# A fused attention and two-block MoE kernel: attention's TensorE order regrouped by shape, two small jobs moved to GpSimd

## The chip, the cores and the metric

The kernel runs on one core of one Trainium2 chip. The metric is the device time of one execution in microseconds, the median of the runs. Before the change it is 554.88 us (three runs, 554.71 to 554.99).

## The reference

```
scores = q @ k.T / 8            # 2 batches x 12 heads, 448 positions, 64 per head
scores = where(causal, scores, -1e9)
attn   = exp(scores - max);  attn = attn / (sum(attn) + 1e-9)
x      = attn @ v               # -> 896 tokens x 768
y      = ((x @ w_a) * (x @ w_b)) @ w_out          # d_ff 1536
h      = y @ w_in;   out = (h / (1 + exp(-h))) @ w_out2   # d_ff 2048
```

All of it is float32.

## The kernel before

The core does attention first (about 0 to 97 us), then the products of the two MoE blocks, which split every float32 operand into a high and a low part.

**Units and half-units.** Attention works on 12 units: unit `u` is a pair of heads of one batch (6 per batch). The 448 query positions of a unit are three blocks of 128 and a last one of 64. The last blocks of both heads share one tile, called `LAST`. A unit is done in two half-units `(u, i)`: half 0 holds block 1 of both heads and `LAST`, half 1 holds blocks 2 and 0 of both heads (`STEPS`). A half-unit goes through four stages:

- `scores` (L622, L631): products of q and k into PSUM tiles `sc`. L622 has 64 rows by 64 columns of weights, four of them side by side in the array. L631 is the product for `LAST`: its weights `q_last` are padded with zeros to 128 rows, by 64 columns. These two stages, in short S(u,i) and L(u), share the PSUM pool `ps_s`.
- `soft`: on VectorE (DVE) one instruction adds mask and scale and takes the row minimum of the negated scores (L646, tile `sm`, four buffers), then ScalarE (ACT) takes the exponential and its row sums (L651, tiles `p`, `sums`).
- `normalize`: DVE adds 1e-9 to the sums (L659) and takes the reciprocal (L660), then GpSimd (POOL) multiplies `p` by it (L663).
- `transposes`, in short T(u,i): eight 128x128 transposes on TensorE (PE) into two PSUM banks `pt` (L694), the first copied out by ACT, the second by DVE (both L782). Then `pv`: PV(u,i) multiplies with v (L705), weights of 128 rows by 64 columns; when a unit is complete, `arrive` makes `xh` (ACT, L390), for batch 1 also `xf` (ACT, L393), and `xl` (DVE, L397).

**What sets the order.** Everything is in the order in which the program issues it. The loop over steps `d` (two per unit) calls per step, before the change, `scores(d)`, then `pv` of half-unit `d - LAG_PV`, then `transposes` of half-unit `d - LAG_T`. What the other engines have to do is put into the table `late` by `defer(k, prio, fn)`, for step `d + k`, and at the end of a step that step's entries are issued in order of `prio`:

```
for _, fn in sorted(late.pop(d, ()), key=lambda e: e[0]):
    fn()
```

Then `line.to` issues the steps of the weights' conversion that are due. The weights of the first two granules (groups of weight blocks) are converted during attention: `exp` (ACT, L220, scales the upper words), `low` (ACT, L226), `join` and `sign` (DVE, L232 and L237), then the high and low parts (ACT L259, DVE L263). In the last steps the first MoE products ("fill", L302, 36 matmuls in four portions) are put between the attention stages. TensorE starts with eight warm-up matmuls (L723), while the first q and k load.

**PSUM.** `ps_s` has three banks for scores, transposes use two banks `ps_t` and one bank `ps_g[1]` in turn, `ps_x` and `ps_g[0]` hold `xo`.

Of the kernel before, what the change touches and what calls it, by code (L numbers as in the profile page):

```python
# [10 lines left out]
F32 = mybir.dt.float32  # L11
# [7 lines left out]
P = 128  # L19
D = 64  # L20
# [48 lines left out]
def fused_kernel(ctx: ExitStack, tc: tile.TileContext, qk, v, w_ab, w_mid, w_in, w_out, out):  # L69
# [122 lines left out]
    def convert(g):  # L192
# [22 lines left out]
        for i in range(2):  # L215


            @step(due["exp"][i])
            def _(i=i):
                nc.scalar.activation(out=word(i, 1).bitcast(F32), in_=word(i, 1).bitcast(F32), func=AF.Copy,  # L220
                                     scale=2.0 ** -112)


            @step(due["low"][i])
            def _(i=i):
                nc.scalar.activation(out=word(i, 0), in_=word(i, 0), func=AF.Relu, bias=wbias, scale=2.0 ** -29)  # L226

            @step(due["join"][i])
            def _(i=i):
                if i == 0:  # L230
                    g["wq"] = wtp.tile([P, 2 * H], F32, tag="wq", name="wq")
                nc.vector.scalar_tensor_tensor(out=xi(i), in0=word(i, 1), scalar=3, in1=word(i, 0),  # L232
                                               op0=ALU.logical_shift_left, op1=ALU.bitwise_or)

            @step(due["sign"][i])
            def _(i=i):
                nc.vector.scalar_tensor_tensor(out=xi(i), in0=word(i, 1), scalar=0x80000000, in1=xi(i),  # L237
                                               op0=ALU.bitwise_and, op1=ALU.bitwise_or)
                R.free(g["raw"][i])
# [295 lines left out]

    for g in granules:
        if g["stage"] == 3 and g["m"] in (0, 2):
            g["due"] = (CONV_X, CONV_Y)[g["m"] // 2]  # L540
        if g["stage"] == 4 and g["m"] == 0 and not g["fast"] and g["k"]:
            g["due"] = CONV_Z
    loads += [(g, src) for g in granules for src in g["src"]]

    with tc.manual_schedule():

        with ExitStack() as actx:
# [47 lines left out]
            def load_qk(u):  # L595
                t = U[u]
                t["qk"] = qk_p.tile([P, 2, S], F32, tag="qk", name="qk")
                nc.sync.dma_start(out=t["qk"], in_=qk[u])
                for h in range(2):
                    r = slice(h * D, (h + 1) * D)  # L600
                    nc.sync.dma_start(out=q_last[u % NQ][r, h, :], in_=qk[u, r, 0, S - D:])

            def load_v(u):
                U[u]["v"] = v_p.tile([P, NKB, P], F32, tag="v", name="v")
                nc.sync.dma_start(out=U[u]["v"], in_=v[u])

            def scores(u, i):


                t = U[u]  # L610
                if i == 0:
                    for n in ("sums", "nmax", "rcp"):
                        t[n] = st_p.tile([P, len(COL)], F32, tag=n, name=n)
                bank = [ps_s.tile([P, 512], F32, tag="s", name="sc") for _ in range(2)]
                q, k = t["qk"][:, 0], t["qk"][:, 1]
                work, o = [], HS if i == 0 else 0
                for n in (1,) if i == 0 else (2, 0):
                    K = P * (n + 1)
                    for h in range(2):
                        r = slice(h * D, (h + 1) * D)  # L620
                        for e in range(2):
                            nc.tensor.matmul(  # L622
                                out=bank[h][e * D:(e + 1) * D, o:o + K], lhsT=q[r, n * P + e * D:n * P + (e + 1) * D],
                                rhs=k[r, 0:K], start=True, stop=True,
                            )
                        work.append(((h, n), [(bank[h][:, o:o + K], mask[:, 3 * P - K:])]))
                    o += K
                if i == 0:
                    for part in range(2):
                        for h in range(2):  # L630
                            nc.tensor.matmul(  # L631
                                out=bank[part][h * D:(h + 1) * D, 0:HS], lhsT=q_last[u % NQ][:, h, :],
                                rhs=k[:, part * HS:(part + 1) * HS], start=True, stop=True,
                            )
                    work.append((LAST, [(bank[0][:, 0:HS], mask[:, 0:HS]), (bank[1][:, 0:HS], mask_last)]))
                for j, src in work:
                    defer(0, 2, partial(soft, u, j, src))
# [30 lines left out]
            def transposes(u, i):  # L668
# [4 lines left out]
                    t["pt"] = pt_p.tile([P, NKB, 2, S], F32, tag="ptr", name="ptr")  # L673
                bank = []
                for _ in range(2):
                    pool, tag = (ps_g[1], "g") if n_banks[0] % 3 == 2 and u < NP + 2 else (ps_t, "t")
                    n_banks[0] += 1
                    bank.append(pool.tile([P, 512], F32, tag=tag, name="pt"))
                o, todo = [0, 0], []
                for n, copy, kb, nkb, blk in COPIES[i]:  # L680
                    w = D if blk == 3 else P
                    size = nkb * 2 * w
                    src = bank[n][:, o[n]:o[n] + size].rearrange("p (k h q) -> p k h q", k=nkb, h=2)
                    o[n] += size
                    dst = t["pt"][:, kb:kb + nkb, :, blk * P:blk * P + w]
                    for a in range(nkb):
                        for j, out_ in [(LAST, src[:, a])] if blk == 3 else [((h, blk), src[:, a, h]) for h in range(2)]:
                            todo.append((out_, p_sb[u % 2][j][:, (kb + a) * P:(kb + a + 1) * P]))
                    if nkb == 1:
                        src, dst = src[:, 0], dst[:, 0]  # L690
                    copy = nc.vector.tensor_copy if copy == "vector" else nc.scalar.copy
                    defer(1, 0, partial(copy, out=dst, in_=src))
                for out_, p in todo:
                    nc.tensor.transpose(out=out_, in_=p, identity=ident)  # L694

            def pv(u, kb):
# [55 lines left out]
            for d in range(n_steps):  # L752
                now[0] = d
                u, i = divmod(d, 2)
                if u == NU and i == 0:
# [4 lines left out]
                    banks.add(ctx.enter_context(right(name="ps_r", bufs=3, space=PSUM, reuse_waits="tile")), 3)  # L760
# [8 lines left out]
                if u < NU:  # L769
                    scores(u, i)  # L770
                u, i = divmod(d - LAG_PV, 2)
                if 0 <= u < NU:
                    for kb in range(2 * i, min(2 * i + 2, NKB)):
                        pv(u, kb)
                u, i = divmod(d - LAG_T, 2)
                if 0 <= u < NU:
                    transposes(u, i)
# [273 lines left out]
```

## Time and profile before

| | |
|---|---|
| median of three runs | 554.88 us |
| the profiled execution | 554.62 us, of which its span (first to last instruction) 552.8 us |
| TensorE busy | 545.0 us, 99% of the span, at the full granted clock throughout |
| DVE, ACT, POOL busy | 453.7, 382.9, 50.5 us |
| the chain that ended last | PE 96%: MoE products L302 83%, attention's transposes, values and scores 4, 4 and 5% |
| attention, up to the unbroken stream of L302 | 0 to 97.45 us |

The profile's page gives busy time by engine and the chain of waits, which follows the work back from the last instruction. On PE a matmul's end is modelled, so that a busy PE can still hold small gaps: stretches between the starts of neighbouring groups are safer than busy shares. A float32 matmul is recorded as two instructions, so "x8" is four products.

### The profile page before, as it was taken

The page shows a single profiled execution, that of the slowest core. Times are in us where ns is not written, and L with a number is a line of the kernel's source. Part 1 is how long each engine was busy: PE and PEld are TensorE (multiplying, and loading weights), DVE is VectorE, ACT ScalarE, POOL GpSimd, SP SyncE. Part 2 cuts the span into 40 slices and gives each one's busy share as a digit, 9 for nine tenths or more (in the row PEclk, how much of TensorE's full clock was granted, in tenths as well). Part 3 has the DMA queues.
Part 4 walks back from the last instruction along what each step waited for, and adds up shares of the span by engine and source line. Part 5 has one row for each costly group of instructions (what it writes and reads, how often), then busy time and mean ns, then how long its engine had stood idle before and what let it go on. Part 6 is the DMA issues. An engine that isn't in the chain of part 4 may idle for free.

```text
span 552.8 us, 8463 instructions
## 1 busy us (share of the span) xinstructions
PE 545.0 (99%) x3043; PEld 476.1 (86%) x3043; DVE 453.7 (82%) x867; ACT 382.9 (69%) x709; POOL 50.5 (9%) x101
## 2 busy tenths in 40 slices
PE   8999999999999999999999999999999999999997
PEld 5565656999999999999999999999999999999996
DVE  4898989998989898979683788988887698758883
ACT  4979896856666666678563575877777788465731
POOL 3665554000000000000000000000000000000000
PEclk9999999999999999999999999999999999999999
DMA  7436314034343333333333333323224152414122
GB/s 239 154 114 242 104 39 172 2 128 162 122 155 116 117 116 114 116 114 115 114 115 115 114 116 114 115 114 115 114 97 128 63 188 98 149 79 132 58 96 88
DMA packets 17226, 65.82 MB, mean 119 GB/s; under 512 B 3616, under 2 KB 5152, under 8 KB 17184
## 3 DMA queue, kind: packets, MB, share of 16 engines
q1 hardware_dynamic: 17184, 65.28, 34.5%
q8 instruction: 24, 0.39, 0.3%
q14 instruction: 18, 0.15, 0.1%
HBM read 62.52 MB, written 2.75 MB: 118 GB/s over the span
## 4 chain that ended last, share of the span: by engine, by line
PE 96%; DVE 2%; issue 1%; POOL 1%; ACT 0%; POOLq 0%; DVEq 0%
PE acc L302 83%; PE pt L694 4%; PE xo L705 4%; PE sc L622 3%; PE sc L631 2%; DVE sm L646 1%; PE wp L723 1%; POOL p L663 1%; ACT p L651 0%; DVE xf L403 0%; DVE ptr L782 0%; DVE o L895 0%; DVE rcp L660 0%; DVE xl L397 0%; DVE nmax L646 0%
## 5 line engine op out<-in xcount | busy, mean ns | idle before, releaser
L325 ACT COPY s<-acc 128x448 f32<-128x448 f32 x84 | 44.8, 534 | 75.0 <-PE acc L302 74.6
L232 DVE SCALAR_TENSOR_TENSOR wq<-wr 128x768 uint32<-128x768 uint32 (+1 forms) x70 | 65.5, 939 | 19.2 <-ACT wr L226 18.8
L226 ACT ACTIVATE wr<-wr,wbias 128x768 uint32<-128x768 uint32 (+1 forms) x70 | 68.2, 974 | 0.0
L220 ACT ACTIVATE wr<-wr 128x768 f32<-128x768 f32 (+1 forms) x70 | 62.7, 895 | 2.3 <-DMA wr<-w_mid 1.1
L237 DVE SCALAR_TENSOR_TENSOR wq<-wr,wq 128x768 uint32<-128x768 uint32 (+1 forms) x70 | 63.3, 931 | 0.1
L651 ACT ACTIVATE p<-sm,nmax 128x256 f32<-128x256 f32 (+3 forms) x84 | 43.8, 525 | 13.0 <-DVE nmax L646 7.2
L663 POOL TENSOR_SCALAR p<-p,rcp 128x256 f32<-128x256 f32 (+3 forms) x84 | 47.7, 587 | 37.6 <-ACT p L651 19.1
L646 DVE CUSTOM_DVE_ANT_0 sm<-sc,mask 128x256 f32<-128x256 f32 (+3 forms) x84 | 30.4, 414 | 11.2 <-PE sc L631 7.1
L302 PE MATMUL acc<-th,wgbl 128*128 128x448 f32 x132 | 38.6, 366 | 0.0
L302 PE MATMUL acc<-th,wgal 128*128 128x448 f32 x132 | 38.5, 366 | 0.0
L302 PE MATMUL acc<-th,wgbh 128*128 128x448 f32 x132 | 38.5, 366 | 0.0
L302 PE MATMUL acc<-tl,wgbh 128*128 128x448 f32 x132 | 38.5, 365 | 0.0
L302 PE MATMUL acc<-tl,wgah 128*128 128x448 f32 x132 | 38.5, 365 | 0.0
L302 PE MATMUL acc<-th,wgah 128*128 128x448 f32 x132 | 38.4, 365 | 0.0
L830 DVE TENSOR_TENSOR s<-acc,s 128x448 f32<-128x448 f32 x42 | 25.9, 618 | 5.2 <-PE acc L302 5.2
L694 PEld LDWEIGHTS pt<-ident,p 128*128 128x128 f32 x192 | 20.5, 140 | 10.2 <-POOL p L663 8.1
L694 PE MATMUL pt<-ident,p 128*128 128x128 f32 x192 | 27.4, 281 | 1.8 <-POOL p L663 1.3
L302 PEld LDWEIGHTS acc<-th,wgbh 128*128 128x128 f32 x132 | 24.8, 188 | 2.2 <-DVE s L830 0.2
L302 PEld LDWEIGHTS acc<-th,wgah 128*128 128x128 f32 x132 | 24.8, 188 | 2.2
L302 PEld LDWEIGHTS acc<-th,wgbl 128*128 128x128 f32 x132 | 24.8, 188 | 2.0
L302 PEld LDWEIGHTS acc<-th,wgal 128*128 128x128 f32 x132 | 24.8, 188 | 2.0
L302 PEld LDWEIGHTS acc<-tl,wgbh 128*128 128x128 f32 x132 | 24.8, 188 | 1.9
(182 smaller groups left out, 1455.5 us busy)
## 6 DMA issues: line engine op xcount, KB each, us to landing
wr<-w_ab SPq DMA_DIRECT2D x24, 768.0 KB, 5.0
wr<-w_in SPq DMA_DIRECT2D x16, 768.0 KB, 4.5
wr<-w_mid SPq DMA_DIRECT2D x12, 768.0 KB, 5.0
wr<-w_out SPq DMA_DIRECT2D x12, 768.0 KB, 5.2
qk<-qk SPq DMA_DIRECT2D x12, 448.0 KB, 4.1
v<-v SPq DMA_DIRECT2D x12, 256.0 KB, 3.2
wr<-w_out SPq DMA_DIRECT2D x6, 512.0 KB, 4.2
out<-o SPq DMA_DIRECT2D x12, 224.0 KB, 2.0
```

The source lines that it names most:

```text
L220: nc.scalar.activation(out=word(i, 1).bitcast(F32), in_=word(i, 1).bitcast(F32), func=AF.Copy, scale=2.0 ** -112)
L226: nc.scalar.activation(out=word(i, 0), in_=word(i, 0), func=AF.Relu, bias=wbias, scale=2.0 ** -29)
L232: nc.vector.scalar_tensor_tensor(out=xi(i), in0=word(i, 1), scalar=3, in1=word(i, 0), op0=ALU.logical_shift_left, op1=ALU.bitwise_or)
L237: nc.vector.scalar_tensor_tensor(out=xi(i), in0=word(i, 1), scalar=0x80000000, in1=xi(i), op0=ALU.bitwise_and, op1=ALU.bitwise_or)
L302: nc.tensor.matmul(out=acc[:, 0:S], lhsT=w, rhs=a, start=first, stop=last, skip_group_check=True)
L325: nc.scalar.copy(out=t, in_=acc[:, 0:S])
L646: nc.vector.tensor_tensor_reduce(out=sm[:, o:o + m.shape[-1]], in0=sc, in1=m, op0=ALU.add, op1=ALU.min, scale=-(D ** -0.5), scalar=nmax, a ...
L651: nc.scalar.activation(out=p_sb[u % 2][j][:, 0:K], in_=sm[:, 0:K], func=AF.Exp, bias=t["nmax"][:, c:c + 1], scale=-1.0, accum_out=t["sums" ...
L663: nc.gpsimd.tensor_scalar(out=pj, in0=pj, scalar1=t["rcp"][:, COL[j]:COL[j] + 1], scalar2=1.0, op0=ALU.mult, op1=ALU.mult,)
L694: nc.tensor.transpose(out=out_, in_=p, identity=ident)
L705: nc.tensor.matmul(out=t["x"][h * D:(h + 1) * D, kb * P:S], lhsT=t["v"][:, kb, h * D:(h + 1) * D], rhs=t["pt"][:, kb, h, kb * P:S], start= ...
L830: nc.vector.tensor_tensor(out=t, in0=bank[:, 0:S], in1=other, op=ALU.add)
```

## The change

Four things are changed together.

1. The order on TensorE. In an odd step it is now PV of the half-unit `d - 6`, L of the *next* unit (`scores_last`), T of `d - 3`, S(u,1); in an even step S(u,0), T of `d - 3`, PV of `d - 6`. So S(u,1) and S(u+1,0) are neighbours, and so are PV(u',0), PV(u',1) and L. `LAG_T` and `LAG_PV` grow by one, and the loop has 31 steps where it had 30. L of a unit now stands before its S(u,0), in the same PSUM banks.
2. PSUM banks and priorities. `ps_s` has four banks; transposes have one bank `ps_t` and one bank `ps_g[1]`, so each of the two is used by every half-unit. The copies out of `pt` are issued in the step of their transposes with priority 1, behind S(u,0)'s `soft` and ahead of S(u,1)'s.
3. GpSimd adds the 1e-9, and does the `exp` step of the first two granules' conversion (four instructions).
4. For unit 0, `q_last` is copied from the loaded tile by ACT and DVE, where two small DMAs did it; its `soft` is issued at once.

```diff
-LAG_T = 2
-LAG_PV = 5
+LAG_T = 3
+LAG_PV = 6
...
-                nc.scalar.activation(out=word(i, 1).bitcast(F32), in_=word(i, 1).bitcast(F32), func=AF.Copy,
-                                     scale=2.0 ** -112)
+                w = word(i, 1).bitcast(F32)
+                if g["early"]:
+                    nc.gpsimd.tensor_scalar(out=w, in0=w, scalar1=2.0 ** -112, scalar2=1.0, op0=ALU.mult, op1=ALU.mult)
+                else:
+                    nc.scalar.activation(out=w, in_=w, func=AF.Copy, scale=2.0 ** -112)
...
-            ps_s = sctx.enter_context(right(name="ps_s", bufs=3, space=PSUM))
+            ps_s = sctx.enter_context(right(name="ps_s", bufs=4, space=PSUM))
...
-            ps_t = actx.enter_context(tc.tile_pool(name="ps_t", bufs=2, space=PSUM))
+            ps_t = actx.enter_context(tc.tile_pool(name="ps_t", bufs=1, space=PSUM))
...
+                    for h in range(2):
+                        todo = partial(soft, u, (h, n), [(bank[h][:, o:o + K], mask[:, 3 * P - K:])])
+                        if u == 0:
+                            todo()
+                        else:
+                            defer(0, 2 if i else 0, todo)
...
+            def scores_last(u):
+                t = U[u]
+                if "x01" not in t:
+                    t["x01"] = banks_of(u, 0)
+                bank, k = t["x01"], t["qk"][:, 1]
...
+                defer(0, 0 if u else 3, partial(
+                    soft, u, LAST, [(bank[0][:, 0:HS], mask[:, 0:HS]), (bank[1][:, 0:HS], mask_last)]))
...
-                nc.vector.tensor_scalar_add(out=t["sums"][:, cs], in0=t["sums"][:, cs], scalar1=1e-9)
+                nc.gpsimd.tensor_scalar(out=t["sums"][:, cs], in0=t["sums"][:, cs], scalar1=1e-9, scalar2=1.0,
+                                        op0=ALU.add, op1=ALU.mult)
...
-                    pool, tag = (ps_g[1], "g") if n_banks[0] % 3 == 2 and u < NP + 2 else (ps_t, "t")
+                    pool, tag = (ps_g[1], "g") if n_banks[0] % 2 else (ps_t, "t")
...
-                    defer(1, 0, partial(copy, out=dst, in_=src))
+                    defer(0, 1, partial(copy, out=dst, in_=src))
...
+                u, i = divmod(d + 1, 2)
+                if i:
+                    half(scores, d)
+                    if d == 0:
+                        scores_last(0)
+                    half(transposes, d - LAG_T)
+                    half(pv_half, d - LAG_PV)
+                else:
+                    half(pv_half, d - LAG_PV)
+                    if 1 < d and u < NU:
+                        scores_last(u)
+                    half(transposes, d - LAG_T)
+                    half(scores, d)
+                    if d == 1:
+                        scores_last(u)
```

TensorE, most of one unit in the steady part, before (`p_0`, `p_1` and `p_2` are block 1 of both heads and `LAST`, `p_3` to `p_6` blocks 2 and 0; the last number tells even from odd units):

```order
L622 MATMUL sc<-qk 64x256 x4
L631 MATMUL sc<-qk,q_116 64x224 x4
L705 MATMUL xo<-ptr,v 64x192 x2
L705 MATMUL xo<-ptr,v 64x64 x2
L694 MATMUL pt<-ident,p_0_119 128x128
L694 MATMUL pt<-ident,p_1_120 128x128
L694 MATMUL pt<-ident,p_0_119 128x128
L694 MATMUL pt<-ident,p_1_120 128x128
L694 MATMUL pt<-ident,p_2_121 128x128 x4
L622 MATMUL sc<-qk 64x384 x4
L622 MATMUL sc<-qk 64x128 x4
L705 MATMUL xo<-ptr,v 64x448 x2
```

The same part of the program on TensorE with the change (L632 is S, L652 is L, L715 is T, L726 is PV):

```order
L726 MATMUL xo<-ptr,v 64x192 x2
L726 MATMUL xo<-ptr,v 64x64 x2
L652 MATMUL sc<-qk,q_118 64x224 x4
L715 MATMUL pt<-ident,p_0_126 128x128
L715 MATMUL pt<-ident,p_1_127 128x128
L715 MATMUL pt<-ident,p_0_126 128x128
L715 MATMUL pt<-ident,p_1_127 128x128
L715 MATMUL pt<-ident,p_2_128 128x128 x4
L632 MATMUL sc<-qk 64x384 x4
L632 MATMUL sc<-qk 64x128 x4
L632 MATMUL sc<-qk 64x256 x4
L715 MATMUL pt<-ident,p_3_129 128x128
```

The 256-column scores of the next unit moved behind the 384 and 128-column ones of this unit, and L moved behind the end of PV.

ScalarE, about one unit, before (L651 the exponentials, L782 the copies out of `pt`):

```order
L651 ACTIVATE p_3_122,sums<-sm,nmax 128x384 [waits DVE_49,Pool_49]
L651 ACTIVATE p_4_123,sums<-sm,nmax 128x384 [waits DVE_49,Pool_49]
L651 ACTIVATE p_5_124,sums<-sm,nmax 128x128 [waits DVE_49,Pool_49]
L651 ACTIVATE p_6_125,sums<-sm,nmax 128x128 [waits DVE_49,Pool_49]
L782 COPY ptr<-pt 128x4x128 [waits PE_49]
L651 ACTIVATE p_0_126,sums<-sm,nmax 128x256 [waits DVE_49,Pool_49]
L651 ACTIVATE p_1_127,sums<-sm,nmax 128x256 [waits DVE_49,Pool_49]
L651 ACTIVATE p_2_128,sums<-sm,nmax 128x448 [waits DVE_49,Pool_49]
L782 COPY ptr<-pt 128x4x128 [waits PE_49,Activation_49]
L390 CAST xh<-xo 128x448
```

ScalarE with the change (L671 the exponentials, L819 the copies, L393 `xh`):

```order
L671 ACTIVATE p_3_122,sums<-sm,nmax 128x384 [waits DVE_49]
L671 ACTIVATE p_4_123,sums<-sm,nmax 128x384 [waits DVE_49]
L671 ACTIVATE p_5_124,sums<-sm,nmax 128x128 [waits DVE_49]
L671 ACTIVATE p_6_125,sums<-sm,nmax 128x128 [waits DVE_49]
L671 ACTIVATE p_0_126,sums<-sm,nmax 128x256 [waits DVE_49]
L671 ACTIVATE p_1_127,sums<-sm,nmax 128x256 [waits DVE_49]
L393 CAST xh<-xo 128x448
L819 COPY ptr<-pt 128x4x128 [waits PE_49]
L671 ACTIVATE p_2_121,sums<-sm,nmax 128x448 [waits DVE_49,PE_49,Pool_49]
L819 COPY ptr<-pt 128x4x128 [waits Activation_49]
```

The copy of T(u-2,1) moved behind six exponentials and `xh`, and the exponential of `LAST` moved behind it.

TensorE, the start of T(u,0) and what its instructions wait for, before:

```order
L694 MATMUL pt<-ident,p_0_119 128x128 [waits Pool_49]
L694 MATMUL pt<-ident,p_1_120 128x128 [waits Pool_49]
L694 MATMUL pt<-ident,p_0_119 128x128
L694 MATMUL pt<-ident,p_1_120 128x128
L694 MATMUL pt<-ident,p_2_121 128x128 [waits DVE_49,PE_49,Pool_49]
```

And with the change:

```order
L715 MATMUL pt<-ident,p_0_119 128x128 [waits Activation_49,Pool_49]
L715 MATMUL pt<-ident,p_1_120 128x128 [waits Pool_49]
L715 MATMUL pt<-ident,p_0_119 128x128
L715 MATMUL pt<-ident,p_1_120 128x128
L715 MATMUL pt<-ident,p_2_121 128x128 [waits DVE_49,PE_49,Pool_49]
```

The first transpose of every half-unit now waits for ACT's copy of the half-unit before.

## Rows read from the trace of the kernel before

**Rows 1.** The page: busy us by engine, share of the span, instructions.
```profile
PE 545.0 (99%) x3043; PEld 476.1 (86%) x3043; DVE 453.7 (82%) x867; ACT 382.9 (69%) x709; POOL 50.5 (9%) x101
```

**Rows 2.** Busy us by engine in units 3 and 11 and the end of attention.
```profile
19.55:26.07 6.52, 6.52 (x70) 4.05 (x68) 4.99 (x24) 6.52 (x21) 3.79 (x9) 1.00 0.38 117
...
72.77:79.75 6.98, 6.57 (x65) 3.89 (x65) 5.80 (x26) 6.98 (x21) 3.92 (x8) 1.00 0.14 42
79.75:97.45 17.70, 16.80 (x113) 11.98 (x109) 17.43 (x38) 12.34 (x27) 7.29 (x10) 1.00 0.39 134
```

**Rows 3.** The chain that ended last: start, us, what; an S(u,1), one unit, another S(u,0).
```profile
25.04 1.02 PE sc L622 x16
...
48.84 0.59 PE sc L622 x8
49.43 0.91 PE sc L631 x8
50.34 0.44 PE xo L705 x8
50.78 1.02 PE pt L694 x8
51.80 1.02 PE sc L622 x16
52.83 1.44 PE xo L705 x8
...
61.75 0.88 PE sc L622 x8
```

**Rows 4.** DVE's timeline: start, us, what, idle before; the first L646 of S(0,1), S(3,1).
```profile
8.95 0.56 DVE L646 CUSTOM_DVE_ANT_0 sm<-sc,mask 128x384 f32<-128x384 f32 x1 [0.48 <-PE sc L622]
...
26.10 0.56 DVE L646 CUSTOM_DVE_ANT_0 sm<-sc,mask 128x384 f32<-128x384 f32 x1 [0.25 <-PE sc L622]
...
27.78 0.94 DVE L232 SCALAR_TENSOR_TENSOR wq<-wr 128x768 uint32<-128x768 uint32 x1
```

**Rows 5.** ACT's timeline: an exponential behind its sm, then a stretch without idle time.
```profile
9.55 0.61 ACT L651 ACTIVATE p<-sm,nmax 128x384 f32<-128x384 f32 x1 [0.28 <-DVE nmax L646]
...
70.61 0.51 ACT L651 ACTIVATE p<-sm,nmax 128x256 f32<-128x256 f32 x1
...
73.73 0.53 ACT L390 CAST xh<-xo 128x448 fp32r<-128x448 f32 x1
74.15 0.54 ACT L393 COPY xf<-xo 128x448 f32<-128x448 f32 x1
74.58 0.63 ACT L651 ACTIVATE p<-sm,nmax 128x384 f32<-128x384 f32 x1
...
76.56 1.00 ACT L226 ACTIVATE wr<-wr,wbias 128x768 uint32<-128x768 uint32 x1
77.45 0.57 ACT L782 COPY ptr<-pt 128x512 f32<-128x512 f32 x1
```

**Rows 6.** PE's timeline: a T that waits for ACT's copy of its bank.
```profile
78.17 0.63 PE L694 MATMUL pt<-ident,p 128*128 128x128 f32 x4 [0.41 <-ACT ptr L782]
```

**Rows 7.** Groups by form, 0 to 100 us: count, busy us, mean ns, idle before.
```profile
L663 POOL TENSOR_SCALAR p<-p,rcp 128x384 f32<-128x384 f32 x24 | 17.8, 753 | 18.2 <-DVE rcp L660 13.8 <-ACT p L651 4.4
...
L397 DVE TENSOR_TENSOR xl<-xo,xh 128x448 fp32r<-128x448 f32 x12 | 7.2, 599 | 0.0
...
L232 DVE SCALAR_TENSOR_TENSOR wq<-wr 128x768 uint32<-128x768 uint32 x4 | 4.3, 1075 | 0.0
...
L259 ACT CAST wgah<-wq 128x768 fp32r<-128x768 f32 x2 | 1.7, 830 | 0.0
```

**Rows 8.** The same view from 100 to 549 us, where GpSimd is idle.
```profile
L232 DVE SCALAR_TENSOR_TENSOR wq<-wr 128x768 uint32<-128x768 uint32 x60 | 57.2, 955 | 18.6 <-ACT wr L226 18.2
```

**Rows 9.** PE's timeline: S(1,1), and T(11,0) behind GpSimd.
```profile
13.09 1.09 PE L622 MATMUL sc<-qk 64*64 64x384 f32 x16
...
85.78 1.06 PE L694 MATMUL pt<-ident,p 128*128 128x128 f32 x8 [0.80 <-POOL p L663]
```

More of the change, by code (lines that the diff above doesn't have):

```diff
@@ L534, in fused_kernel @@
         granule([w_out[m + i, :, N4:] for i in range(2)], NP, True, stage=4, m=m)
-    for g in granules:
+    for at, g in enumerate(granules):
+        g["early"] = at < 2
         if g["stage"] == 3 and g["m"] in (0, 2):
@@ L598, in load_qk @@
                 nc.sync.dma_start(out=t["qk"], in_=qk[u])
-                for h in range(2):
+                for h, copy in enumerate((nc.scalar.copy, nc.vector.tensor_copy)):
                     r = slice(h * D, (h + 1) * D)
-                    nc.sync.dma_start(out=q_last[u % NQ][r, h, :], in_=qk[u, r, 0, S - D:])
+                    if u == 0:
+                        copy(out=q_last[u][r, h, :], in_=t["qk"][r, 0, S - D:])
+                    else:
+                        nc.sync.dma_start(out=q_last[u % NQ][r, h, :], in_=qk[u, r, 0, S - D:])
             def load_v(u):
@@ L605, in load_v, with banks_of @@
                 nc.sync.dma_start(out=U[u]["v"], in_=v[u])
+            def banks_of(u, i):
+                if i == 0:
+                    for n in ("sums", "nmax", "rcp"):
+                        U[u][n] = st_p.tile([P, len(COL)], F32, tag=n, name=n)
+                return [ps_s.tile([P, 512], F32, tag="s", name="sc") for _ in range(2)]
             def scores(u, i):
                 t = U[u]
[L611 to L614, printed above, removed]
+                bank = t["x01"] if i == 0 else banks_of(u, i)
                 q, k = t["qk"][:, 0], t["qk"][:, 1]
-                work, o = [], HS if i == 0 else 0
+                o = HS if i == 0 else 0
                 for n in (1,) if i == 0 else (2, 0):
@@ L625, in scores @@
                             )
-                        work.append(((h, n), [(bank[h][:, o:o + K], mask[:, 3 * P - K:])]))
-                    o += K
[L628 to L637, printed above, removed]
+                    for h in range(2):
+                        todo = partial(soft, u, (h, n), [(bank[h][:, o:o + K], mask[:, 3 * P - K:])])
+                        if u == 0:
+                            todo()
+                        else:
+                            defer(0, 2 if i else 0, todo)
+                    o += K
+            def scores_last(u):
[3 more added lines that the diff above has]
+                bank, k = t["x01"], t["qk"][:, 1]
+                for part in range(2):
+                    for h in range(2):
+                        nc.tensor.matmul(
+                            out=bank[part][h * D:(h + 1) * D, 0:HS], lhsT=q_last[u % NQ][:, h, :],
+                            rhs=k[:, part * HS:(part + 1) * HS], start=True, stop=True,
+                        )
+                defer(0, 0 if u else 3, partial(
+                    soft, u, LAST, [(bank[0][:, 0:HS], mask[:, 0:HS]), (bank[1][:, 0:HS], mask_last)]))
             def soft(u, j, src):
@@ L710, in pv, with pv_half @@
                     defer(1, 1, partial(finish, b, chunk, t["x"][:, 0:S]))
+            def pv_half(u, i):
+                for kb in range(2 * i, min(2 * i + 2, NKB)):
+                    pv(u, kb)
             def finish(b, chunk, src):
-                defer(XL_STEPS, 4, arrive(b, chunk, src))
+                defer(XL_STEPS, 5, arrive(b, chunk, src))
                 if b == 1 and chunk % 2:
-                    defer(XL_STEPS, 5, lambda: sums_x.gens.append(sums_of(chunk // 2)))
+                    defer(XL_STEPS, 6, lambda: sums_x.gens.append(sums_of(chunk // 2)))
             wz = const.tile([P, P], F32, name="wz")
@@ L759, in fused_kernel @@
                     W.add(ctx.enter_context(right(name="wring1", bufs=RING2, reuse_waits="tile")), RING2)
[L760 removed]
+                    banks.add(ctx.enter_context(right(name="ps_r", bufs=4, space=PSUM, reuse_waits="tile")), 4)
                 if i == 0 and 0 < u and u + 2 < NU:
@@ L768, in fused_kernel, with half @@
                     done_fill += 1
[L769 to L777, printed above, removed]
+                def half(fn, at):
+                    if 0 <= at < 2 * NU:
+                        fn(*divmod(at, 2))
+                u, i = divmod(d + 1, 2)
+                if d == 0:
+                    U[0]["x01"] = banks_of(0, 0)
+                if i:
+                    half(scores, d)
+                    if d == 0:
+                        scores_last(0)
+                    half(transposes, d - LAG_T)
+                    half(pv_half, d - LAG_PV)
+                else:
+                    half(pv_half, d - LAG_PV)
[5 more added lines that the diff above has]
+                        scores_last(u)
                 u, i = divmod(d - 1, 2)
                 if 0 <= u < NU:
-                    defer(0, 3, partial(normalize, u, i))
+                    defer(0, 4, partial(normalize, u, i))
                 for _, fn in sorted(late.pop(d, ()), key=lambda e: e[0]):
@@ L793, in fused_kernel @@
         A.add(ctx.enter_context(tc.tile_pool(name="slots2", bufs=A3, reuse_waits="tile")), A3)
-        banks.add(ctx.enter_context(tc.tile_pool(name="ps_m", bufs=3, space=PSUM, reuse_waits="tile")), 3)
+        banks.add(ctx.enter_context(tc.tile_pool(name="ps_m", bufs=2, space=PSUM, reuse_waits="tile")), 2)
         for p in ps_g:
```

## The prediction

> **What bounds the kernel now.** I read the page's busy shares first [rows 1]: TensorE is busy 99% of the span, the others have room on average. The change touches attention alone, so I took the stretches between the ends of neighbouring S(u,1) next [rows 2]. Unit 3 took 6.52 us, unit 11 took 6.98, and the nine units 3 to 11 together 79.75 - 19.55 = 60.20 us (6.69 each); 17.70 us later begins the unbroken stream of L302. In unit 3 ACT shows no idle time, in unit 11 neither, so ACT is nearly as full as PE; that is the fact on which I decide. The chain of waits then shows one unit on PE group by group [rows 3]: S(u,0) 0.59, L 0.91, the second PV half 0.44, T 1.02, S(u,1) 1.02, the first PV half 1.44, T 1.02, sum 6.44 us. Units that take longer wait for something: in unit 9 S(u,0) lasts 0.88, which is 0.29 of waiting for a scores bank (four units have it).
>
> **The new order on PE.** S(u,0) and the second PV half stream the same 256 columns, yet take 0.59 and 0.44 [rows 3]. The first follows a T, whose weights have another shape, the second follows L, which has its own shape. So a change of shape costs about 0.15 us. Before there are six changes per unit, after four: T, then PV, PV and L as one block, T, then S and S. PE's own work falls from 6.44 to 6.44 - 2 x 0.15 = 6.14 us per unit. This step alone would be worth 9 x 0.30 = 2.7 us, and the fourth scores bank another 4 x 0.29 = 1.2.
>
> **The new loop through ACT.** T has now one bank `ps_t`, emptied by ACT, and the next T cannot start before that copy ends. The copy of T(u-2,1) stands on ACT behind the four exponentials of S(u-1,1), the two of S(u,0), and `xh`. These cannot start before S(u-1,1) is computed. And the next T, T(u-1,0), stands on PE in front of S(u,1). So there is a loop from the end of S(u-1,1) to the end of S(u,1). Its pieces:
> - S(u,1) ends, DVE's first `sm` starts: S(3,1) ends at 25.04 + 1.02 = 26.06 [rows 3], `sm` starts at 26.10 [rows 4]: 0.04.
> - from there to its exponential: 8.95 [rows 4] to 9.55 [rows 5]: 0.60.
> - four exponentials 74.58 to 76.56 = 1.98 [rows 5]; two of 256 columns at 0.51 = 1.02 [rows 5].
> - `xh` 73.73 to 74.15 = 0.42; `xf`, for batch 1 only, 74.15 to 74.58 = 0.43 [rows 5].
> - the copy's start to the waiting T's start: 77.45 [rows 5] to 78.17 [rows 6]: 0.72.
> - T without a change in front of it (that is over while PE waits) 1.02 - 0.15 = 0.87, then S(u,1) 1.02 [rows 3].
>
> The loop is 0.04 + 0.60 + 1.98 + 1.02 + 0.72 + 0.87 + 1.02 = 6.25 us without `xh`, 6.67 with it, 7.10 with `xf`. PE alone would reach T(u-1,0) after S(u,0) 0.44, T 1.02, PV 1.44 + 0.44, L 0.91 - 0.15 and a change 0.15, at 4.25; ACT lets it start at 4.78 with `xh`. So PE waits about half a microsecond in most units, and the two saved changes of shape are lost in that wait. The copy as last on ACT is what decides: DVE's copy of the other bank comes earlier.
>
> **What else stands in the loop.** Conversion steps issued between the exponentials and the copy lengthen it. On ACT two casts L259 at 0.73 (0.83 [rows 7] less the 0.1 by which neighbouring rows overlap), in units 7 and 8, and one L226 at 0.89 (76.56 to 77.45 [rows 5]) in unit 11. On DVE a `join` before S(4,0)'s `sm` and a `sign` behind `xl` before S(6,0)'s. The four `sm`, sum and reciprocal take 26.10 to 27.78 = 1.68 [rows 4], less 0.17 for the add that leaves; with 0.94 for the `join` and 0.5 for `sm` to exponential, ACT could start those two at 0.04 + 1.51 + 0.94 + 0.5 = 2.99, and is free at 2.62: +0.4 in unit 4. With `xl`, 0.5 (0.599 [rows 7] less the overlap), +0.9 in unit 6. The other L226 of the early granules come behind the copy and are hidden by ACT's wait for T.
>
> The units then take: unit 3 6.25; units 4 to 9 6 x 6.67 = 40.02; units 10 and 11 2 x 7.10 = 14.20; extras 0.4 + 0.9 + 2 x 0.73 + 0.89 = 3.65. Sum 64.12 against 60.20: **+3.9 us**.
>
> **Start and tail.** S(1,1) ends at about 14.2 before [rows 9]; the change starts DVE earlier but puts `soft` of L(1) ahead of the first reciprocal, so I leave that point within 0.2. From there S(2,1) took to 19.55 before, since no loop bound it; with the loop it is 14.2 + 0.2 + 6.25 = 20.65: **+1.1**, bounds 0 and +1.5. In the tail the four portions of fill lie in the same places, T(11,0) no longer waits 0.80 for GpSimd [rows 9], because its half-unit has a step more: **-0.8**. DVE is busy 17.43 of those 17.70 us [rows 2], so bounds are -1.6 and +1.5.
>
> **The smaller edits.** The add of 1e-9 takes 24 instructions off DVE, which no longer sets the end anywhere but in the tail, and puts each in front of the reciprocal that follows on DVE. For half-unit 0 its inputs are ready long before; for half-unit 1 it queues behind three multiplications, as late as DVE comes to the reciprocal anyway. Behind it on DVE stands only `soft` of L(u+1), which has until the end of T. I take 0, bounds 0 and +1.5 (one early scaling in front of it); a gain is excluded, because DVE waits for PE or ACT there. The four scalings of 128x768 leave ACT, so none of them is in the sum of the loop. On GpSimd one takes between 0.75 (a multiplication of 384 columns [rows 7]) and twice that; I take 1.5, since it has twice the columns. GpSimd has over 2 us free per unit (3.79 busy in 6.52 [rows 2]). The first unit's copies of `q_last` run behind the warm-up matmuls; two fewer DMAs at SP's start bring the next loads earlier, nothing waits for them.
>
> GpSimd's work does slow DVE: `join` takes 1.075 us here [rows 7] and 0.955 where GpSimd is idle [rows 8], 0.12 each. The Trainium skill ("SBUF — State Buffer", section "Who interferes with whom") says that a DVE instruction with two SBUF inputs and a GpSimd instruction that reads SBUF exclude each other for a whole instruction. By that, a `join` could stand behind a whole scaling; here the rows show a tenth of it on average.
>
> **The sum.** +3.9 + 1.1 - 0.8 = +4.2 us on the profiled execution's 554.62, so 558.8. That execution lies 0.26 below the median of 554.88; on the median's footing I predict **559.1 us**.
>
> **Rivals.**
> - *ACT's chain does not bind, PE does.* If the copy is done by the time PE comes (the exponentials start earlier, or DVE sets them off sooner than my rows), units take 6.14: 9 x 6.14 = 55.3 against 60.20, -4.9; tail -0.8, start +0.5: 549.7 on the median's footing. For it: before, T waited for ACT's copy once, for 0.41 [rows 6]. Against: all pieces of the loop are measured rows, in series, and half of the 0.53 would have to go before a unit is shorter than 6.4. It decides when T(u-1,0) starts by 4.25 behind S(u-1,1). The Trainium skill ("TensorEngine Tiling (Array Packing)", "Key Properties") says that a change of tiling mode drains TensorE; the 0.15 agrees, and by that rule alone the change is a gain. Chance 0.24.
> - *The loop binds, but the extras are hidden and the start costs nothing*: 9 units at 60.5, tail -0.8: 554.4, no change. Chance 0.08.
> - *GpSimd holds DVE.* Four scalings of up to 1.5, each with a DVE step behind it that sits in the loop: up to 6 more, 565; that is what the Trainium skill's rule of "SBUF — State Buffer" would do at its worst. Against: 0.12 in the rows. Chance 0.04.
> - *The neighbours save nothing*, as weights of equal shape still cost the change. Then PE needs 6.44 per unit, still under the loop's 6.67; each T starts as late, and the time stays within 0.5 of my forecast. Against: the 0.44. Chance 0.04.
>
> **How the numbers follow.** Forecast, with the fourth rival inside it, 0.64; its own range, with the loop off by 0.1 per unit and the bounds of start and tail, is 555.5 to 562. 0.2%, or 1.1 us, is about what a measurement of this kernel can tell from no change. Faster by more: 0.24, the first rival. Within: the second, 0.08. Slower: 0.64 + 0.04 = 0.68. The range 550.5 to 562.0 leaves out half of the first rival's runs at most and the third, under 0.2.
>
> **What would show it.** Right: units 3 to 11 at 6.7 to 8 us, PE idle at T(u-1,0) about 0.5 us in each with ACT's copy as releaser (rows "PE pt ... ACT ptr" of several us in all, 0.4 before), PV and L as one block without a gap, ACT's exponentials without a pause up to the copy. Wrong: units near 6.15 and no wait of pt on ACT. The start would be wrong if S(2,1) ends before 20; the extras if units 7 and 8 are as short as 9. The forecast falls if the first exponential starts within 0.2 us of the end of S(u,1), or if DVE, held by the reciprocal's wait for GpSimd, is the releaser instead.

## The result and the profile after

The changed kernel takes **562.39 us** (561.38 to 564.09, four runs) against 554.80 (554.48 to 554.99) on the same chip: ratio 1.0141, interval 1.0111 to 1.017, slower by 7.6 us. The forecast was 559.1, the range ended at 562.0. The profiled execution took 563.21, its span 561.4, which is 8.6 more than before's 552.8.

The page of the kernel after: busy time by engine, then the chain that ended last (before it was 96% PE).
```profile
PE 542.8 (97%) x3043; PEld 474.8 (85%) x3043; DVE 450.3 (80%) x844; ACT 379.6 (68%) x706; POOL 57.5 (10%) x129
...
PE 85%; DVE 7%; ACT 5%; issue 1%; POOL 1%; DVEq 0%; ACTq 0%; POOLq 0%
```
PE's busy time falls by 2.2 us [rows 1], and yet the chain now goes through DVE and ACT for 12%. PE waits; its list of waits up to 115 us (us in total, times, longest) says for what:
```profile
PE pt L715 <- ACT ptr L819: 5.4, 5, 2.0
PE xo L726 <- DVE xl L400: 4.5, 7, 0.7
PE pt L715 <- POOL p L684: 1.4, 3, 0.6
```
The first row is the forecast wait (0.41 before [rows 6]). It is longer than listed: three more waits of T, 0.21, 0.60 and 0.29, stand under GpSimd's name, but there too T starts 0.70 to 0.73 behind the start of ACT's copy, as in the five waits of the first row. One of them, ACT's copy and then PE's T:
```profile
56.07 0.57 ACT L819 COPY ptr<-pt 128x512 f32<-128x512 f32 x1
```
```profile
56.78 1.07 PE L715 MATMUL pt<-ident,p 128*128 128x128 f32 x8 [0.60 <-POOL p L684]
```
So ACT's copy holds T for about 6.5 us. The second row was not in the forecast. One unit on PE's timeline (start, duration, what; idle time before and its releaser), from S(8,1) to S(9,1), with the T in front of it:
```profile
64.34 1.06 PE L715 MATMUL pt<-ident,p 128*128 128x128 f32 x8 [0.61 <-ACT ptr L819]
65.34 1.53 PE L632 MATMUL sc<-qk 64*64 64x384 f32 x24
66.82 1.07 PE L715 MATMUL pt<-ident,p 128*128 128x128 f32 x8
68.58 1.95 PE L726 MATMUL xo<-ptr,v 128*64 128x448 f32 x16 [0.69 <-DVE xl L400]
70.36 0.93 PE L652 MATMUL sc<-qk,q 128*64 128x224 f32 x8
71.22 1.09 PE L715 MATMUL pt<-ident,p 128*128 128x128 f32 x8
72.25 1.53 PE L632 MATMUL sc<-qk 64*64 64x384 f32 x24
```
The same unit on ACT and on DVE:
```profile
67.06 0.62 ACT L671 ACTIVATE p<-sm,nmax 128x384 f32<-128x384 f32 x1 [0.34 <-DVE nmax L666]
...
70.03 0.51 ACT L393 CAST xh<-xo 128x448 fp32r<-128x448 f32 x1
70.44 0.58 ACT L819 COPY ptr<-pt 128x512 f32<-128x512 f32 x1
```
```profile
66.46 0.56 DVE L666 CUSTOM_DVE_ANT_0 sm<-sc,mask 128x384 f32<-128x384 f32 x1 [0.33 <-PE sc L632]
...
67.94 0.59 DVE L400 TENSOR_TENSOR xl<-xo,xh 128x448 fp32r<-128x448 f32 x1
```
Two loops run here side by side. **Through ACT**, as forecast: S(8,1), `sm`, four and two exponentials, `xh`, the copy, T(8,0), S(9,1). **Through DVE**: PV starts `xo` in one of two banks, which must first be emptied by the `xl` of two units before. That `xl` stands on DVE behind the four `sm` of the same S(8,1): 65.34 + 1.12 (first `sm`) + 1.48 (to `xl`) + 0.64 (to PV) + 1.78 (PV) + 0.86 (L) + 1.03 (T) = 72.25. In this unit the second loop is the longer one, by less than 0.1 us.

The starts of S(u,1), u = 2 to 11, are 22.23, 28.63, 35.66, 42.58, 50.22, 57.78, 65.34, 72.25, 79.49 and 87.65. So the span's 8.6 us come from four stretches:

| stretch | before | after | difference | forecast |
|---|---|---|---|---|
| to the end of S(2,1) | 19.55 | 23.25 | +3.7 | +1.1 |
| units 3 to 11 | 60.20 | 65.42 | +5.2 | +3.9 |
| to the unbroken stream of MoE products | 17.63 | 16.52 | -1.1 | -0.8 |
| the rest | 455.4 | 456.2 | +0.8 | 0 |

Here the stream begins where PE's timeline has its first product, at 97.38 before and 105.19 after. Of the last row, 0.40 is one wait. It stands at the same place, with 0.39 to 0.41, in six of the other kernels with the new order and with 0.2 in two; in the remaining three and in the old order it isn't seen. The rest of the row I can't place:
```profile
137.23 0.47 PE L305 MATMUL acc<-p3h,wdh 128*128 128x448 f32 x1 [0.40 <-ACT s L328]
```

### The profile page after: what moved, and what is told of

It is laid out like the page before. It is cut to its first block, busy times and chain, and to the rows that moved or that the text cites. A ratio compares the mean times of both kernels' runs of the same rounds, so it can differ in the third digit from the quotient of the medians.

```text
span 561.4 us, 8394 instructions
## 1 busy us (share of the span) xinstructions
PE 542.8 (97%) x3043; PEld 474.8 (85%) x3043; DVE 450.3 (80%) x844; ACT 379.6 (68%) x706; POOL 57.5 (10%) x129
## 4 chain that ended last, share of the span: by engine, by line
PE 85%; DVE 7%; ACT 5%; issue 1%; POOL 1%; DVEq 0%; ACTq 0%; POOLq 0%
PE acc L305 76%; PE sc L632 3%; PE pt L715 2%; ACT p L671 2%; PE xo L726 2%; PE sc L652 1%; DVE wq L240 1%; POOL p L684 1%; DVE sm L666 1%; DVE xl L400 1%; DVE S L418 1%; PE wp L748 1%; DVE wq L235 1%; ACT ptr L819 1%; ACT wr L229 0%
## 5 line engine op out<-in xcount | busy, mean ns | idle before, releaser
L224 ACT ACTIVATE wr<-wr 128x768 f32<-128x768 f32 (+1 forms) x66 | 59.1, 895 | 1.6 <-DMA wr<-w_mid 1.2
L671 ACT ACTIVATE p<-sm,nmax 128x256 f32<-128x256 f32 (+3 forms) x84 | 43.7, 521 | 21.8 <-DVE nmax L666 11.6
L666 DVE CUSTOM_DVE_ANT_0 sm<-sc,mask 128x256 f32<-128x256 f32 (+3 forms) x84 | 31.7, 415 | 9.8 <-PE sc L632 6.6
L715 PEld LDWEIGHTS pt<-ident,p 128*128 128x128 f32 x192 | 20.7, 140 | 15.5 <-POOL p L684 6.7
L715 PE MATMUL pt<-ident,p 128*128 128x128 f32 x192 | 25.6, 276 | 7.5 <-ACT ptr L819 5.4
L726 PE MATMUL xo<-ptr,v 128*64 128x448 f32 (+3 forms) x192 | 23.6, 386 | 4.5 <-DVE xl L400 4.5
```

Of the source, the lines that this page charges most:

```text
L224: nc.scalar.activation(out=w, in_=w, func=AF.Copy, scale=2.0 ** -112)
L666: nc.vector.tensor_tensor_reduce(out=sm[:, o:o + m.shape[-1]], in0=sc, in1=m, op0=ALU.add, op1=ALU.min, scale=-(D ** -0.5), scalar=nmax, a ...
L671: nc.scalar.activation(out=p_sb[u % 2][j][:, 0:K], in_=sm[:, 0:K], func=AF.Exp, bias=t["nmax"][:, c:c + 1], scale=-1.0, accum_out=t["sums" ...
L726: nc.tensor.matmul(out=t["x"][h * D:(h + 1) * D, kb * P:S], lhsT=t["v"][:, kb, h * D:(h + 1) * D], rhs=t["pt"][:, kb, h, kb * P:S], start= ...
```

## Experiments

"Difference" is the median less that of the kernel before in the same session. The ratio is taken over all executions and not from the two medians, so it can differ from them by up to 0.25%. One execution of kernel 13 (1380 us) was disturbed and is left out; that kernel was run again for its profile.

| kernel | us | difference | ratio, interval |
|---|---|---|---|
| the change | 562.39 | +7.6 | 1.0141, 1.0111 to 1.017 |
| 1 ACT's copy early | 556.44 | +2.1 | 1.0043, 1.0023 to 1.0063 |
| 2 `xl` early | 562.07 | +7.7 | 1.0115, 1.0077 to 1.0153 |
| 3 both | 553.78 | -0.6 | 0.9993, 0.9976 to 1.0009 |
| 4 start | 561.75 | +7.4 | 1.0121, 1.0087 to 1.0156 |
| 5 no GpSimd edits | 565.60 | +11.3 | 1.0197, 1.0178 to 1.0215 |
| 6 scalings back on ACT | 566.14 | +11.4 | 1.0199, 1.0179 to 1.022 |
| 7 add back on DVE | 563.04 | +8.3 | 1.0148, 1.0131 to 1.0165 |
| 8 both, add on DVE | 553.82 | -0.5 | 1.0003, 0.9986 to 1.002 |
| 9 both, add on DVE, start | 553.22 | -1.1 | 0.9979, 0.9969 to 0.9988 |
| 10 as 9, reciprocal early | 554.39 | -0.3 | 0.9983, 0.9966 to 1.0 |
| 11 both, start | 553.22 | -1.5 | 0.9967, 0.9952 to 0.9982 |
| 12 before + add on GpSimd | 552.80 | -1.9 | 0.9965, 0.9954 to 0.9977 |
| 13 before + both GpSimd edits | 552.45, again 553.00 | -1.9, -1.7 | 0.9965, 0.9953 to 0.9978; again 0.9965, 0.9952 to 0.9978 |
| 14 before + scalings on GpSimd | 554.44 | -0.3 | 0.9996, 0.9987 to 1.0006 |

**1, 2, 3: the two loops.** The theory was that ACT's copy sets the loop and that a second loop through `xl` stands right behind it; the rival, that one of them alone does it. Kernel 1:
```
-                    defer(0, 1, partial(copy, out=dst, in_=src))
+                    defer(0, -1 if i and copy == nc.scalar.copy else 1, partial(copy, out=dst, in_=src))
```


> Only ACT's copy of T(u,1) is issued ahead of the two exponentials of S(u+2,0) and of xh; everything else is as in the changed kernel (562.4). If the loop through ACT's copy alone sets the unit, it shrinks by two exponentials and xh (0.99 + 0.42 us) and the unit falls from 6.4-8.2 to what PE needs, about 6.2-6.4: nine units 57-59 instead of 65.4, time 554-556. If the second loop (PV's bank emptied by xl on DVE, behind four sm) is as long as the first, units 5 to 11 keep 6.9 or so and only those without xl, or with a conversion on ACT, gain: time 560-562, and PE's wait on ACT's copy is gone while its wait on xl grows from 4.5 us to 6 or more.

Kernel 2, and kernel 3 with both edits:
```
-                defer(XL_STEPS, 5, arrive(b, chunk, src))
+                defer(XL_STEPS, 1, arrive(b, chunk, src))
```


> Only xl is issued on DVE ahead of the copy and the four sm of S(u,1) instead of behind them. If the loop through DVE's xl sets the unit, units 5 to 11 fall toward 6.2-6.4: time 555-558. If the ACT loop is nearly as long (6.84 against 6.91 in unit 9), the wait on xl goes from 4.5 us to about 0, the wait on ACT's copy grows by nearly as much, and the time stays within 1 us: 561.5-562.5.

> Both reorderings together. If two nearly equal loops bind, the gain is more than the sum of the two alone: units near 6.2-6.5, nine units 56-58.5, time 553-556, with both waits near 0. If a third chain (GpSimd's normalization into T, or sm into the exponentials) comes right behind, units stay at 6.6-6.8 and the time at 558-560. The late start (S(2,1) ends at 23.3 instead of 19.6) stays in either case.

Kernel 1 gains 5.5 us, more than I expected of it with the second loop there; kernel 2 gains nothing that can be measured; both together gain 8.2. So the loop through ACT's copy is the main cause, and the loop through `xl`, which sets two units of the change, counts only when the first is cut, where it is worth another 2.7. The profiles agree: units 3 to 11 take 61.06 us in kernel 1 and 65.42 in the change, and the stretch from S(1,1) to S(2,1) 5.52 and 6.50, together 5.3. The waits of kernel 1, of kernel 2 and of kernel 3 on PE:
```profile
PE xo L726 <- DVE xl L400: 3.9, 6, 0.7
...
PE pt L715 <- ACT ptr L819: 0.5, 1, 0.5
```
```profile
PE pt L715 <- ACT ptr L819: 8.6, 7, 2.4
```
```profile
PE pt L715 <- POOL sums L679: 2.4, 5, 0.7
PE pt L715 <- ACT ptr L819: 1.4, 3, 0.6
```
In kernel 1 the copy has nearly gone, in kernel 2 it takes over what `xl` left, in kernel 3 both are small. Units 3 to 11 take 58.73 us there (20.71 to 79.44) against before's 60.20. A unit of kernel 3 in which PE shows no wait, from S(3,1) on:
```profile
26.35 1.53 PE L632 MATMUL sc<-qk 64*64 64x384 f32 x24
...
32.58 1.67 PE L632 MATMUL sc<-qk 64*64 64x384 f32 x24
```
That is 6.23 us, where the old order needs 6.44 [rows 3]. So the two saved changes of shape exist and are worth 0.2 us per unit (the shortest such unit, in kernel 9, takes 6.18). The Trainium skill ("TensorEngine Tiling (Array Packing)", "Key Properties") says that a change of tiling mode drains TensorE; the trace agrees, at about 0.1 us for each.

**4: the start.** The theory was that the first unit's `soft`, issued between its scores, makes PE's writes to one part of a PSUM bank wait for DVE's reads of another part.
```
                         if u == 0:
-                            todo()
+                            defer(0, -1, todo)
```


> The order of instructions is that of the changed kernel on every engine; only the first unit's soft steps are issued behind its last scores, so that TensorE's writes of one part of a bank no longer wait for DVE's reads of another part of it. If those waits are the late start (0.73, half of 1.76, 0.66, 0.26 us on PE before 13.7), S(2,1) ends 2 to 2.6 us earlier, at about 21, and the time falls by as much, to 560. If the loop is started by something else (the first T waits for GpSimd and ACT), S(2,1) still ends after 22.5 and the time stays at 561.5-562.4.

The time is 0.2 to 0.6 us less, which the scatter of these runs can't tell from nothing: mostly a miss. The profile shows why one execution says little here (windows of this kernel: us, length, PE busy, granted clock, DMA share, GB/s):
```profile
8.00:10.00 2.00, 0.86 (x8) 1.00 1.01 415
10.00:12.00 2.00, 2.00 (x12) 0.68 0.95 361
12.00:14.00 2.00, 2.00 (x14) 0.50 0.41 150
```
PE waited 1.14 us in the first window for DVE, and behind it the granted clock fell, to 0.50 from 12 to 14 us, the level of 1.2 GHz. In the changed kernel the start also ran slowly for a while, and in kernel 1, whose instructions are the same there, it did not. PE's timeline of the change, then of kernel 1, then of the kernel before:
```profile
6.63 1.76 PE L652 MATMUL sc<-qk,q 128*64 128x224 f32 x8 [0.73 <-DVE nmax L666]
8.32 1.56 PE L632 MATMUL sc<-qk 64*64 64x384 f32 x8
...
15.73 1.53 PE L632 MATMUL sc<-qk 64*64 64x384 f32 x24
...
21.24 1.06 PE L715 MATMUL pt<-ident,p 128*128 128x128 f32 x8 [1.54 <-ACT ptr L819]
22.23 1.53 PE L632 MATMUL sc<-qk 64*64 64x384 f32 x24
```
```profile
6.45 0.98 PE L652 MATMUL sc<-qk,q 128*64 128x224 f32 x8 [0.74 <-DVE nmax L666]
7.36 0.88 PE L632 MATMUL sc<-qk 64*64 64x384 f32 x8
8.88 0.91 PE L632 MATMUL sc<-qk 64*64 64x128 f32 x8 [0.66 <-DVE nmax L666]
...
10.96 1.25 PE L632 MATMUL sc<-qk 64*64 64x256 f32 x8 [0.26 <-DVE part L666]
12.15 0.98 PE L652 MATMUL sc<-qk,q 128*64 128x224 f32 x8
...
14.08 1.53 PE L632 MATMUL sc<-qk 64*64 64x384 f32 x24
...
18.61 1.06 PE L715 MATMUL pt<-ident,p 128*128 128x128 f32 x8 [0.55 <-ACT ptr L819]
19.60 1.53 PE L632 MATMUL sc<-qk 64*64 64x384 f32 x24
```
```profile
8.02 1.21 PE L622 MATMUL sc<-qk 64*64 64x384 f32 x16 [0.26 <-DVE part L646]
10.35 0.65 PE L622 MATMUL sc<-qk 64*64 64x256 f32 x4 [1.12 <-DVE nmax L646]
```
The same L(0) took 1.76 and 0.98. So of the start's +3.7 us, S(1,1) is late by 15.73 - 13.09 = 2.64 [rows 9]: 15.73 - 14.08 = 1.65 for the slower matmuls, and 0.99 that kernel 1 has as well. Most of the 0.99 isn't a wait. It is L(2), at 12.15 in kernel 1, which the new order puts in front of S(1,1): the T behind it starts at 13.06, 0.91 later. The waits for DVE in front of S(1,1) are 0.74 + 0.66 + 0.26 = 1.66, but the kernel before had 0.26 + 1.12 = 1.38 of them, so they add 0.28. The other groups are together 0.2 shorter. From S(1,1) to S(2,1) it takes 6.50 us, in kernel 1 5.52, before 5.4 [rows 2, 9]: the loop's 1.1, with the wait on ACT's copy at 1.54 and 0.55.

**5, 6, 7: the GpSimd edits undone in the changed kernel.** The edits are those of the change's diff, backwards.

> The changed kernel with both GpSimd edits undone (1e-9 on DVE, all scalings on ACT). If the scalings then stand in the ACT loop, up to four times 0.9 us: 563-566. If the adds on GpSimd were what made the chain long (T waits for GpSimd), faster: 560-561.5. If neither matters: 561.5-562.5.

> The changed kernel (562.4) with the early scalings alone back on ACT, the add stays on GpSimd. Undoing both edits cost about 3 us. If it is the scalings, which then stand between the exponentials and the copy that T waits for, 564.5 to 566. If it is the add, 562 to 562.8.

> The changed kernel with the add alone back on DVE, the scalings stay on GpSimd. If the ACT loop hides whatever DVE saves, 562 to 563, as in the changed kernel. If DVE's loop through xl, with two more instructions of 0.17 to 0.43 us per unit in front of xl, sets units 5 to 10, 564 to 565.5. If the crossing to GpSimd is what costs, 560 to 561.5.

Undoing the scalings costs 3.8 us in the median and 2.7 between the fastest runs (564.09, 561.38), undoing the add 0.7, both together 3.7. ACT's timeline of kernel 6 shows the mechanism, a scaling between the exponentials and the copy that PE waits for, and PE's timeline the T behind it:
```profile
26.41 0.39 ACT L671 ACTIVATE p<-sm,nmax 128x128 f32<-128x128 f32 x1
26.79 0.92 ACT L224 ACTIVATE wr<-wr 128x768 f32<-128x768 f32 x1
27.61 0.49 ACT L671 ACTIVATE p<-sm,nmax 128x256 f32<-128x256 f32 x1
...
28.60 0.56 ACT L819 COPY ptr<-pt 128x512 f32<-128x512 f32 x1
```
```profile
29.30 1.06 PE L715 MATMUL pt<-ident,p 128*128 128x128 f32 x8 [1.03 <-POOL p L684]
```
The profile names GpSimd, but T starts 0.70 behind the start of the copy, as in the change. Unit 3 takes 7.22 us there (S(2,1) at 23.08, S(3,1) at 30.30) instead of 6.40. That is the one scaling of four that plainly lengthens a unit, by 0.82. Of the 3.3 us by which the span is longer than the change's (564.7, 561.4), another 0.9 lies between S(1,1) and S(2,1) and 1.6 between the starts of S(11,1) and of the unbroken stream, both where the granted clock was lower (0.50 to 0.53 from 12 to 18 us, 0.69 from 88 to 92). So 0.8 is shown as the price of the scalings, and the rest went with a slower TensorE; whether the scalings set that off is not shown. In kernel 7 PE's wait on `xl` grows from 4.5 to 6.4 us and that on the copy falls from 5.4 to 3.6: DVE's loop takes over, at nearly the same length.

**12, 13, 14: the GpSimd edits alone, in the old order.**

> The kernel before (554.3 on this chip) with only the two GpSimd edits, its TensorE order untouched. If they cost nothing, as the prediction had it, 554.0 to 554.8. If ACT, which is nearly full, gives back the four scalings it loses (0.9 us each), up to 3 us faster: 551.5. If the reciprocal's wait for GpSimd's add holds DVE (it stood for 4.0 us in all in the changed kernel), up to 2 us slower: 556.

> The kernel before with both GpSimd edits, for a profile of an undisturbed execution. 552.2 to 552.8. If the four scalings were in ACT's way, the stretches between S(u,1) that hold them (units 10 and 11, which took 6.5 to 7 us) are shorter by 0.3 to 0.9 each and T's wait of 0.41 on ACT is gone; if it is the tail, T's wait of 0.80 on GpSimd there is shorter.

> The kernel before with the add of 1e-9 alone on GpSimd. The changed order with both reorderings showed no difference between the add on GpSimd and on DVE (553.78 and 553.82), so 554.0 to 554.7 if that holds here. If DVE's lighter load is what gained 1.8 us, 552.5 to 553.

> The kernel before with the early scalings alone on GpSimd. If ACT is what limits, 552.4 to 552.8, all of the gain. If the add makes the gain, 554.0 to 554.7.

Here it is the other way about: the add alone gains 1.9 us, the scalings nothing that can be measured. PE's timeline shows where: S(5,0), waiting for a scores bank, in the kernel before and with the add on GpSimd:
```profile
41.65 0.95 PE L622 MATMUL sc<-qk 64*64 64x256 f32 x8
42.53 0.98 PE L631 MATMUL sc<-qk,q 128*64 128x224 f32 x8
```
```profile
41.67 0.72 PE L622 MATMUL sc<-qk 64*64 64x256 f32 x8
42.32 0.98 PE L631 MATMUL sc<-qk,q 128*64 128x224 f32 x8
```
The bank comes 0.23 earlier, because DVE, which shows no pause here, has two instructions less per unit. Units 3 to 11 together take 59.01 us (18.77 to 77.78), 60.20 before. In the tail T(11,0)'s wait of 0.80 on GpSimd [rows 9] becomes 0.20 on ACT.

**8 to 11: can the new order win?** Each has both reorderings; 8 has the add on DVE, 9 also the edit of 4, 10 also `defer(0, 0.5 if i else 4, partial(normalize, u, i))`, 11 is 9 with the add on GpSimd.

> Both reorderings (553.8) and the add of 1e-9 back on DVE; the early scalings stay on GpSimd. In the run with both reorderings T(u,1) waits 0.24 to 0.75 us, in seven units, for the chain sums, add, reciprocal, normalization. If the add's two crossings between engines make that wait, it goes, about 2.5 us in all: 551-552. If GpSimd's normalization itself is late, the wait stays: 553.5-554.

> As the run before this one, and the first unit's soft steps behind all its scores as in the fourth run. If the start is bound by the same-bank waits, 1 to 2 us less than without it. If DVE's chain and the loop bind the start, the same time within 0.5 us, with the waits only moved later.

> The kernel of all reorderings (553.2), with the second half's sum and reciprocal ahead of DVE's copies of T(u,1). T(u,1) waited there 0.24 to 0.74 us in eight units, 3.6 us in all, for the chain exponentials, reciprocal, normalization. If the order on DVE makes that chain late, 1 to 3 us go: 550.2 to 552. If DVE is simply full (it shows no pause from 57 to 71 us), the time stays at 552.8 to 553.5.

> Both reorderings and the later soft steps of the first unit, with the add on GpSimd as in the changed kernel: what the kernel of 553.2 is with the add back on GpSimd. If DVE, which shows no pause from 57 to 71 us there, is what is full, the lighter DVE gives 551.5 to 552.7. If the crossing gives back what DVE saves, 553 to 553.7.

The add makes no difference between 3 and 8 (its releaser's name changes, the wait stays), and the edit of the start gains 0.6 to 0.9 by the medians. In the profiles of 8 and 9 it takes PE's waits for DVE in front of S(1,1) from 1.66 to 1.13 us and S(1,1) from 14.35 to 13.84. The early reciprocal gains nothing: units 3 to 11 take 59.68 us, in kernel 9 58.68, and T(u,1) still waits, 0.24 to 0.74 us. One such row:
```profile
61.10 1.06 PE L714 MATMUL pt<-ident,p 128*128 128x128 f32 x8 [0.74 <-issue]
```
What ends those waits isn't settled; the order of the reciprocal on DVE is not it. Kernels 9 and 11 beat the kernel before, by 0.2 and 0.3%, and so do 12 and 13, with the old order and the GpSimd edits, by 0.35%. So the new order, mended, is no better than the old one with one line changed.

## Why the prediction was wrong

- **Right: direction and mechanism.** "The copy as last on ACT is what decides": kernel 1 moves that copy alone and takes back 5.5 of 7.6 us. T(u-1,0) waits for it in seven of units 3 to 11, 0.2 to 0.7 us in six of them and 1.96 in unit 11; half a microsecond in most units was forecast. PE's own work was forecast at 6.14 us per unit; the freest units of kernels 3 and 9 show 6.23 and 6.18.
- **Undersized: the loop's pieces.** Unit 8 was put at 7.40 and took 7.56. The first `sm` comes 1.12 after the start of S(u,1), not 1.06, and a T that waited takes 1.00 to the next S (64.34 to 65.34), not 0.87. A T that did not wait, at 71.22, takes 1.03, so the wait hides next to nothing of the change of shape, which I had taken off in full. That is 0.19 in a unit like this one. The seven units that ACT's loop sets are together 0.8 longer than forecast, of the 65.42 - 64.12 = 1.3 in all. The extras, 0.4 in unit 4 and 0.9, 0.73 and 0.73 in units 6 to 8, came out well: the measured units 3 to 11 are 6.40, 7.03, 6.92, 7.64, 7.56, 7.56, 6.91, 7.24 and 8.16, against 6.25, 7.07, 6.67, 7.57, 7.40, 7.40, 6.67, 7.10 and 7.99.
- **Missed: the loop through `xl`.** I followed the bank of T and not that of `xo`. It sets units 5 and 9, which are 0.25 longer than forecast (the other 0.5 of the 1.3), and it alone keeps kernel 1 from being as fast as before.
- **The step that failed: the start**, "I leave that point within 0.2". S(1,1) came 2.64 later in the profiled execution. L(2), which the new order puts in front of S(1,1), was in no term, and takes 0.91. I had seen that the first unit's `soft` is issued early and took it for a gain; the waits for DVE grew by 0.28 instead. And PE's matmuls were slow until about 10 us, 1.65, which was in no term either; what slowed them stays open: kernel 1, with the same instructions and waits there, did not show it.
- **How the misses add up.** On the profiled execution the start is 2.6 longer than forecast, the units 1.3, the MoE part 0.8, the tail 0.3 shorter: 4.4 in all. The median lies 0.4 beyond the range, so with any one of the three at its forecast the time would have lain inside; the start is the largest. Whether the other executions had the slow matmuls isn't known. Without them the profiled one would have taken 563.21 - 1.65 = 561.56, inside the range, and two of the other three took 561.38 and 561.58.
- **The GpSimd edits.** "A gain is excluded, because DVE waits" was said of the new order, where the add is worth 0.7, within what the runs scatter. Of the old order it would be wrong: there DVE frees the bank that S(u,0) waits for (the 0.29 that I had read myself), and the add gains 1.9 us. That GpSimd would hold DVE was a rival at 0.04. It is not borne out: the four `join` steps take 0.938 us on average (1.075 before [rows 7]), undoing the scalings made the kernel slower, and though DVE's reciprocal waited 4.0 us in all for the add, undoing that made it no faster. I had missed the other direction: GpSimd's three multiplications from 31.48 us take 2.09, with a `join` on DVE from 31.23 to 32.16, and those from 38.51, with none, 1.54. A scaling on GpSimd takes 0.91 us, not 1.5.
- **The rest**: the tail's -0.8 was -1.1; the 0.8 in the MoE part was in no term.

## What to carry to other kernels

When a change gives one stage fewer buffers, follow every buffer of that loop, not only the one that shrank: a second loop of nearly the same length hides behind the first, and taking either away alone understates both. Before moving work between engines ask which engine sets the unit in that order; the add was worth 1.9 us in one order and 0.7 in the other, the scalings nothing that can be measured in the first and 2.7 to 3.8 in the second, of which 0.8 is placed. When work moves ahead in the order, count what now stands in front of the first unit. An order on TensorE that saves 0.2 us per unit is worth only what the engines that feed it have in hand.

## What was not expected of the hardware

- The page's granted clock did not show the slow start: the windows of 6 to 10 us read 1.00 in the changed kernel, while L(0), recorded as eight instructions, took 1.76 us against 0.98. In kernel 6 an L takes 1.76 us too, from 12.10, where the granted clock reads 0.50. Durations of equal matmuls show the slow start where the clock's column doesn't.
- The same wait can end with or without a lower clock. T(10,0) waits 1.96 us for ACT in the changed kernel and in kernel 6. In the first the product behind S(11,1) takes 0.47 us, in kernel 6 0.74:
```profile
88.67 0.47 PE L305 MATMUL acc<-xh,wgah 128*128 128x448 f32 x1
```
```profile
91.05 0.74 PE L305 MATMUL acc<-xh,wgah 128*128 128x448 f32 x1
```
  The granted clock of kernel 6 from 90 to 100 us is 0.85. The change and kernels 1 to 8 scatter over 2.1 to 5.3 us (the change 561.4 to 564.1, kernel 2 560.4 to 565.7), kernels 9 to 11, with both reorderings and the edit of the start, over 0.9 to 1.4. The kernel before gave 554.5 to 555.0 in the session of the change (553.9 to 555.4 in the others, but for a few runs at 557.8).
